# Block-sparse attention and a feed-forward layer: queries and choices transposed together by one DMA, two slots ahead

## The chip, the cores and the metric

The kernel runs on one core of a Trainium2 chip. The metric is the time of one execution on the device in microseconds (us); lower is better. TensorE (PE in the profile), VectorE (DVE), ScalarE (ACT), GpSimd (POOL) and SyncE (SP) each run their own instruction stream in program order; DMA transfers are issued from the queues of SP, ACT and POOL and run on 16 DMA engines.

## The reference

```
B, H, S, D = 4, 8, 768, 64;  chunks of 32 keys: nc = 24;  top_k = 6
k_min, k_max = min, max of k over each chunk
ub = sum over D of max(q * k_min, q * k_max)             # a bound for each query and chunk
ub = -1e9 where the chunk lies after the query's own chunk
top_chunks = the 6 chunks with the highest ub
scores = q @ k.T / sqrt(D), -1e9 outside the chosen chunks and after the query
attn = softmax(scores);  x = attn @ v                    # as 3072 tokens x 512
out = relu(x @ w_in) ** 2 @ w_out                        # w_in 512 x 2048, w_out 2048 x 512
```

## The kernel before

The work is cut into eight half batches (384 queries of one of the four batches, `ORDER`, so called hb below, 0 to 7), and each of them into four pairs of heads: 32 pairs, numbered from 0, `s = 4 * hb + p`. The Python loop over `slots` (one turn is called a slot here) writes every engine's instruction order out by hand; no scheduler moves anything. The short names of the code are steps of one pair:

- `step_P`: what the choice needs of the queries. Up to half batch 2 keys and queries are transposed on PE (`step_T`, L252); from half batch 3 on (`ON_PE = 3`) by DMA transposes into the tile `kqT` (`tr`, L305, three of 512 columns for k and three for q in each half batch), and `relus` (L301, L302) makes relu(-q) and relu(q) from it on DVE. The minima and maxima over key chunks come from `step_K` (L321, L327), cut into six parts that `k1()` lays into the slots.
- `step_U`: the bound ub on PE (L352, L356), the eight highest of each row on DVE (L363), and the choice (L364): a tile `nsel` with 1 for each chunk that is not chosen.
- `step_V`: `nsel` of two heads, 128 columns wide, is transposed on PE (L391, two or three 128x128 transposes) and copied by DVE into the query rows (L395, L396). The first four pairs have it together with the queries (L380, L385).
- `step_E`: scores. In the tile `kq` a head has 128 rows: 64 of queries or keys, and 64 where choices on the query side meet, on the key side, a code with -2^24 in the row of the key's chunk. One matmul (L409) thus gives the score and the mask; ACT takes the exponential (L414) and POOL cuts the diagonal blocks (L418).
- `step_F`: attention times v on PE (L434), divided by the sums into x on DVE (L443, L444).
- `step_X`: x of a whole half batch is transposed into `xT`, from half batch 2 to 6 by three DMA transposes on SP (L484), then `push` queues the feed-forward units: `ffn_up` (L524, L528, L530) and `ffn_down` (L540, and the output copy L546 on ACT). `f1()` takes the next unit from that queue; the slots are laid out with `f1()` calls between the attention's steps, so that PE always has something to run.

In a slot s of half batch 3 and later, the order is: (p = 0: `step_F` of the pair before, `step_X`), first scores of s, feed-forward units, `go(s, 2)` (two of the loads due), the other scores of the first head, `step_U(s + 1)`, `step_F(s - 1)`, scores of the second head, `step_V(s + 1)`, `go(s, 99)` (the other loads, `tr`, `place_dma`), the remaining scores, `step_P(s + 2)`, feed-forward units. `place_dma` (L291) copies keys and queries of a half batch from `kqT` into `kq`. Loads of q, k and v go through POOL's queue and are cast to bf16 on the way. SP's queue holds `tr`, x's transposes, `place_dma` and the outputs.

Of the kernel before, what the change touches and what calls it, by code (L numbers as in the profile page):

```python
# [39 lines left out]
def kernel(  # L40
# [36 lines left out]
    qn0 = consts.tile([128, HT, NP, 4, D], BF16, tag="qn0", name="qn")  # L77
# [3 lines left out]
    nsel = [consts.tile([128, HT, 2, D], BF16, tag=f"ns{i}", name="nsel") for i in range(3)]  # L81
    kbds = [consts.tile([128, NP, 2, 2, NC], BF16, tag=f"kbd{i}", name="kbd")
# [27 lines left out]
    def load_q0(h):  # L110
        nc.gpsimd.dma_start(
            out=qn0[:, :, h // 2, 1 + h % 2, :],
            in_=q[0, h, 0:HB].rearrange("(j p) d -> p j d", p=128))
# [39 lines left out]
    for h in (6, 7):  # L153
        load_q0(h)

    oneh = consts.tile([D, S], BF16, tag="oneh")
    nc.vector.tensor_scalar_mul(
        oneh.rearrange("p (c j) -> p c j", j=CH),
        ident[0:D, 0:NC].unsqueeze(2).to_broadcast([D, NC, CH]), OFFSEL)

    def codes(i, half, copy, p0=0, p1=NP):
        for h in range(2):
            copy(kqs[i][SROW[h]:SROW[h] + D, h, p0:p1, 2 * half, :],
                 oneh[:, HB * half:HB * half + HB].unsqueeze(1)
                 .to_broadcast([D, p1 - p0, HB]))

# [20 lines left out]

    def blank(p0, p1, c):

        nc.scalar.mul(qn0[:, :, p0:p1, c, :],  # L190
                      ident[:, 0:D].unsqueeze(1).unsqueeze(1)
                      .to_broadcast([128, HT, p1 - p0, D]), 0.0)

    def clear():

        for h in range(2):
            nc.vector.memset(kqs[1][SROW[h]:SROW[h] + D, h, :, 1, 0:128], 0.0)

# [31 lines left out]
    def step_cast(n, p):  # L230
        if n == "k":
            nc.vector.tensor_copy(packed("k", 0)[:, 2 * p:2 * p + 2], staged["k", p])
        else:
            nc.scalar.copy(qn0[:, :, p, 1:3, :], staged["q", p])

    def step_T(s, kp, qp, ns="kq"):

        b, half, p = slots[s]
        t = st.setdefault(s, {})
        for n in ns:  # L240
            pool, tag = kp if n == "k" else qp
            x = t[n] = pool.tile([128, HB], BF16, tag=tag, name="t" + n)
            if n == "q" and s < NP:
                for j in range(HT):
                    nc.tensor.matmul(
                        x[:, 128 * j:128 * (j + 1)],
                        lhsT=qn0[:, j, p, 1:3, :].rearrange("p h d -> p (h d)"),
                        rhs=ident, is_transpose=True, start=True, stop=True)
                continue
            for hh in range(2):  # L250
                for j in range(TP):
                    nc.tensor.matmul(  # L252
                        x[D * hh:D * hh + D, PP * j:PP * j + PP],
                        lhsT=packed(n, s // NP)[:, 2 * p + hh, D * j:D * j + D],
                        rhs=ident[0:PP, 0:PP], is_transpose=True, start=True, stop=True)
# [19 lines left out]
    def place(s, n, copy, h0=0, h1=2):  # L275
        b, half, p = slots[s]
        for h in range(h0, h1):
            copy(by_token(kqs[b % 2][QROW[h]:QROW[h] + D, h, p, 2 * half + "kq".index(n), :]),
                 in_order(st[s][n][D * h:D * h + D]))
# [67 lines left out]
    def step_U(s):  # L347
        b, half, p = slots[s]
        ncs = 12 * (half + 1)
        j0 = 1 - half  # L350
# [13 lines left out]
        nc.vector.tensor_tensor(  # L364
            (qn0[:, j0:, p, 0:4:3, 0:ncs] if s < NP else nsel[s % 3][:, j0:, :, 0:ncs]),
            ub, m8[:, j0:, :, TOPK - 1:TOPK].to_broadcast([128, HT - j0, 2, ncs]),
            op=ALU.is_lt)

    def qc(s, h):
        b, half, p = slots[s]  # L370
        return kqs[b % 2][:, h, p, 2 * half + 1, :]

    def step_V(s):
        b, half, p = slots[s]
        st[s]["e"] = [None, None]
        if s < NP:
            qt = psA.tile([128, 2, HB], BF16, tag="att", name="qt")
            for hh in range(2):
                for j in range(HT):
                    nc.tensor.matmul(  # L380
                        qt[:, hh, 128 * j:128 * (j + 1)],
                        lhsT=qn0[:, j, p, 2 * hh:2 * hh + 2, :]
                        .rearrange("p h d -> p (h d)"),
                        rhs=ident, is_transpose=True, start=True, stop=True)
            nc.vector.tensor_copy(kqs[b % 2][:, :, p, 2 * half + 1, :], qt)  # L385
            return
        j0 = 1 - half
        c = 128 * j0
        qt = psA.tile([128, HB], BF16, tag="att", name="qt")
        for j in range(j0, HT):  # L390
            nc.tensor.matmul(  # L391
                qt[:, 128 * j:128 * (j + 1)],
                lhsT=nsel[s % 3][:, j].rearrange("p h d -> p (h d)"),
                rhs=ident, is_transpose=True, start=True, stop=True)
        nc.vector.tensor_copy(qc(s, 0)[0:D, c:], qt[0:D, c:])  # L395
        nc.vector.tensor_copy(  # L396
            qc(s, 1)[D:128, c:], qt[D:128, c:])

    def step_E(s, hh, n):
# [7 lines left out]
        for (at, j, i0, m) in BANKS[half][n]:  # L407
            c = 128 * (i0 - HT * half)
            nc.tensor.matmul(  # L409
                ps[:, at:at + 128 * m],  # L410
                lhsT=kqs[b % 2][:, hh, p, 2 * (j // HT), 128 * (j % HT):128 * (j % HT + 1)],
                rhs=qc(s, hh)[:, c:c + 128 * m], start=True, stop=True)
# [11 lines left out]
    def step_F(s, hh):  # L424
# [13 lines left out]
        if hh == 1:  # L438
            if p == 0:
                xs[s // NP] = work.tile([128, HT, DM], BF16, tag="x", name="x")  # L440
# [3 lines left out]
            nc.vector.tensor_mul(  # L444
                x[:, :, 128 * p:128 * (p + 1)].rearrange("p j (h d) -> p h j d", h=2),
                po[:, :, :, 0:D], r.to_broadcast([128, 2, HT, D]))
            st.pop(s)

# [13 lines left out]
    def x_T(hb, g, pt, us=(0, 1)):  # L462
# [3 lines left out]
        for u in us:  # L466
            for j in range(HT):
                nc.tensor.matmul(
                    pts[hb, g][:, u, 128 * j:128 * (j + 1)],
                    lhsT=xs[hb][:, j, 128 * (2 * g + u):128 * (2 * g + u + 1)],  # L470
                    rhs=ident, is_transpose=True, start=True, stop=True)
# [4 lines left out]
    def step_X(hb, pe):  # L476
        xT = xT_of(hb)
        if pe:
            for g in range(2):
                x_T(hb, g, A)  # L480
                x_copy(hb, g, 0, 2, nc.scalar.copy if g else nc.vector.tensor_copy)
        else:
            for j in range(HT):
                nc.sync.dma_start_transpose(  # L484
                    out=xT[:, :, 128 * j:128 * (j + 1)], in_=xs[hb][:, j, :])
        push(hb)
# [46 lines left out]
    def ffn_down(hb, py, t, c, act, tail):  # L533
# [9 lines left out]
        if c == 3:  # L543
            ob = late.tile([128, DM], F32, tag="ob", bufs=3, name="ob")
            if act:
                nc.scalar.copy(ob, py[t])  # L546
# [50 lines left out]
    for g in range(ON_PE, 2 * B):  # L597
# [23 lines left out]
    step_cast("k", 0)  # L621
    blank(0, 1, 0)
    blank(0, 1, 3)
    step_cast("q", 0)
    blank(1, NP, 0)
    clear()
# [3 lines left out]
    step_T2(0)  # L630
    for h in range(2):

        nc.vector.memset(kqs[0][SROW[h]:SROW[h] + D, h, 2, 0, 0:1], 0.0)
    codes(0, 0, nc.sync.dma_start, 2, NP)
    place(0, "k", nc.scalar.copy)
    blank(1, NP, 3)
    step_U(0)
# [9 lines left out]
    extrema(st[1]["k"], 1)  # L647
    for i in range(3):
        nc.vector.memset(nsel[i], 0.0)
    early.close()  # L650
# [40 lines left out]
    for s, (b, half, p) in enumerate(slots):  # L691
# [6 lines left out]
        for fn, *a in first.get(s, ()):  # L698
            fn(*a)
        if ON_PE - 1 <= hb < 2 * B - 1 and p == (2 if hb < ON_PE else 1):  # L700
            parts.extend(step_K(hb + 1))
# [52 lines left out]
        if hb > 1 and s != 2 * NP:  # L754
            f1()
        go(s, 2)
        for n in range(hf, nb):
            step_E(s, 0, n)
        if hb < ON_PE and p:
            k1()  # L760
        if s + 1 < NS:
            step_U(s + 1)
        f1()
        if p and s > NP:
            step_F(s - 1, 0)
            step_F(s - 1, 1)
        if half == 0:
# [5 lines left out]
        f1()  # L773
        if s + 1 < NS:
            step_V(s + 1)
        k1()
        go(s, 99)
        for n in range(hf, nb):
            step_E(s, 1, n)
        k1()  # L780
        if s + 2 < NS:
            step_P(s + 2)
        f1()
        if half == 0:
# [41 lines left out]
```

## Time and profile before

| | |
|---|---|
| median of 3 runs | 278.38 us (276.56 to 282.24) |
| the profiled execution's own time | 278.13 us |
| its span, first to last instruction | 276.4 us |
| TensorE clock granted | 0.999 of full speed |
| DMA | 32.05 MB, 98,272 packets |

The profile is one execution. "Busy" is the time in which an engine had an instruction in work; waits of an engine are listed with the instruction that ended them; the chain is followed back from the last instruction. Rows of a timeline begin with the start and the duration in us. The prediction shows its lines where it uses them.

### The profile page before, as it was taken

The page shows a single profiled execution, that of the slowest core. Times are in us where ns is not written, and L with a number is a line of the kernel's source. Part 1 is how long each engine was busy: PE and PEld are TensorE (multiplying, and loading weights), DVE is VectorE, ACT ScalarE, POOL GpSimd, SP SyncE. Part 2 cuts the span into 40 slices and gives each one's busy share as a digit, 9 for nine tenths or more (in the row PEclk, how much of TensorE's full clock was granted, in tenths as well). Part 3 has the DMA queues.
Part 4 walks back from the last instruction along what each step waited for, and adds up shares of the span by engine and source line. Part 5 has one row for each costly group of instructions (what it writes and reads, how often), then busy time and mean ns, then how long its engine had stood idle before and what let it go on. Part 6 is the DMA issues. An engine that isn't in the chain of part 4 may idle for free.

```text
span 276.4 us, 6695 instructions
## 1 busy us (share of the span) xinstructions
PE 258.0 (93%) x2472; PEld 164.3 (59%) x2497; DVE 168.9 (61%) x647; ACT 181.9 (66%) x400; POOL 90.7 (33%) x135
## 2 busy tenths in 40 slices
PE   7887888899999999999999999999999999999994
PEld 6666555556666566655565566745565566655544
DVE  6878999666994368635884378615883455413411
ACT  5997879588975787835675777825674777625500
POOL 8695356316532017521551116701121111000000
PEclk9999999999999999999999999999999999999999
DMA  7999999959999259995699359997413200111002
GB/s 139 160 205 212 162 213 211 131 69 147 148 188 143 74 117 147 128 156 151 96 169 125 113 104 142 128 129 167 97 60 59 76 2 0 40 39 40 38 38 76
DMA packets 98272, 32.05 MB, mean 116 GB/s; under 512 B 84640, under 2 KB 93984, under 8 KB 98240
## 3 DMA queue, kind: packets, MB, share of 16 engines
q0 software_dynamic: 64688, 14.42, 66.6%
q1 hardware_dynamic: 32464, 16.88, 28.8%
q10 hardware_dynamic: 1088, 0.33, 0.5%
q8 instruction: 19, 0.31, 0.5%
q14 instruction: 13, 0.11, 0.1%
HBM read 27.26 MB, written 6.29 MB: 121 GB/s over the span
## 4 chain that ended last, share of the span: by engine, by line
PE 67%; DMA 9%; DVE 8%; ACT 7%; issue 3%; POOL 3%; SPq 1%; ACTq 0%; POOLq 0%; DVEq 0%
PE py L540 25%; PE ph L524 23%; PE ps L409 9%; PE po L434 7%; DMA vn<-in_v_dram 6%; ACT e L414 2%; ACT ht L528 2%; DVE h L530 2%; DMA xT<-x 2%; DVE km L321 1%; SPq L484 1%; DMA stage<-in_q_dram 1%; POOL e L418 1%; ACT ob L546 1%; PE ub L356 1%
## 5 line engine op out<-in xcount | busy, mean ns | idle before, releaser
L414 ACT ACTIVATE e<-ps 128x512 bf16<-128x512 f32 x192 | 97.1, 551 | 26.5 <-PE ps L409 26.5
L524 PE MATMUL ph<-xT,w_in 128*128 128x384 bf16 x512 | 99.2, 326 | 1.7 <-ACT ht L528 1.0
L540 PE MATMUL py<-w_out,h 128*128 128x512 bf16 x343 | 83.9, 379 | 2.6 <-ACT ob L546 0.9
L528 ACT ACTIVATE ht<-ph 128x384 bf16<-128x384 f32 x128 | 62.7, 500 | 27.5 <-PE ph L524 25.9
L418 POOL TENSOR_SCALAR_AFFINE_SELECT e<-e 128x384 bf16<-128x384 bf16 x64 | 34.1, 539 | 138.2 <-ACT e L414 138.2
L530 DVE TENSOR_TENSOR h<-ht 128x384 bf16<-128x384 bf16 x128 | 46.6, 376 | 43.9 <-ACT ht L528 43.6
L524 PEld LDWEIGHTS <-w_in 128*128 128x128 bf16 x512 | 47.5, 97 | 31.2 <-issue 2.4
L409 PE MATMUL ps<-kq 128*128 128x384 bf16 (+2 forms) x320 | 56.5, 278 | 1.8 <-DVE kq L395 0.8
L540 PEld LDWEIGHTS <-h 128*128 128x128 bf16 x368 | 34.9, 98 | 35.3 <-issue 1.7
L409 PEld LDWEIGHTS <-kq 128*128 128x128 bf16 x320 | 26.4, 98 | 14.5 <-issue 2.6
L434 PEld LDWEIGHTS <-e 128*128 128x128 bf16 x672 | 25.7, 98 | 6.7 <-issue 1.4
L363 DVE MAX8 m<-ub 128x8 f32<-128x24 f32 (+1 forms) x160 | 16.7, 171 | 20.3 <-PE ub L356 19.2
L434 PE MATMUL po<-vn,e 128*128 128x65 bf16 x672 | 27.1, 194 | 2.0 <-POOL e L418 0.8
L546 ACT COPY ob<-py 128x512 f32<-128x512 f32 x19 | 11.1, 586 | 22.7 <-PE py L540 22.3
L444 DVE TENSOR_TENSOR x<-po,r 128x384 bf16<-128x384 f32 x32 | 17.8, 558 | 1.1
L395 DVE COPY kq<-qt 64x384 bf16<-64x384 bf16 (+1 forms) x28 | 8.8, 315 | 12.4 <-PE qt L391 12.4
L105 POOL DMA_DIRECT2D kn<-in_k_dram x15 | 13.3, 891 | 0.6 <-DMA w_out<-in_moe_w_out_dram 0.4
L105 POOL DMA_DIRECT2D qn<-in_q_dram x15 | 13.3, 888 | 0.0
L321 DVE TENSOR_TENSOR km<-km 128x384 bf16<-128x384 bf16 (+3 forms) x40 | 11.3, 283 | 1.1
L356 PE MATMUL ub<-kbd,qr 128*128 128x48 bf16 (+1 forms) x160 | 9.5, 180 | 1.8 <-DVE kbd L219 0.8
L618 PE MATMUL idle<-ident 128*128 128x128 bf16 x97 | 8.7, 252 | 2.4 <-POOL ident masks.py:199 1.4
L121 POOL DMA_DIRECT2D vn<-in_v_dram x12 | 10.7, 904 | 0.4 <-issue 0.4
(68 smaller groups left out, 197.9 us busy)
## 6 DMA issues: line engine op xcount, KB each, us to landing
out_dram<-ob SPq DMA_DIRECT2D x23, 256.0 KB, 2.2
kq<-kqT SPq DMA_DIRECT2D x10, 384.0 KB, 5.2
w_in<-in_moe_w_in_dram POOLq DMA_DIRECT2D x2, 1024.0 KB, 13.2
w_out<-in_moe_w_out_dram POOLq DMA_DIRECT2D x2, 1024.0 KB, 19.7
kn<-in_k_dram POOLq DMA_DIRECT2D x15, 128.0 KB, 5.9
qn<-in_q_dram POOLq DMA_DIRECT2D x15, 128.0 KB, 7.0
vn<-in_v_dram POOLq DMA_DIRECT2D x12, 128.0 KB, 10.6
vn<-in_v_dram POOLq DMA_DIRECT2D x4, 384.0 KB, 7.8
```

The costliest lines, as they stand in the source:

```text
L105: nc.gpsimd.dma_start(out=nat_of(n, g)[:, DM * j:DM * j + DM].rearrange("p (h d) -> p h d", d=D), in_=rows(n, *ORDER[g], 0, H)[:, 128 * j: ...
L321: nc.vector.tensor_tensor(y, x[:, :, :, 0:m], x[:, :, :, m:2 * m], op=op)
L363: nc.vector.max(out=m8[:, j, hh, :], in_=ub[:, j - j0, hh, :])
L409: nc.tensor.matmul(ps[:, at:at + 128 * m], lhsT=kqs[b % 2][:, hh, p, 2 * (j // HT), 128 * (j % HT):128 * (j % HT + 1)], rhs=qc(s, hh)[:, c ...
L414: nc.scalar.activation(e[:, 512 * n + lo:512 * n + hi], ps[:, lo:hi], ACT.Exp, scale=float(scale))
L418: nc.gpsimd.affine_select(out=d, in_=d, compare_op=ALU.is_ge, fill=0.0, base=0, channel_multiplier=-1, pattern=[[0, 3], [1, 128]])
L434: nc.tensor.matmul(po[:, hh, i, :], lhsT=t["e"][hh][:, c:c + 128], rhs=vn[b % 2][:, 2 * p + hh, j, :], start=(j == 0), stop=(j == iq))
L444: nc.vector.tensor_mul(x[:, :, 128 * p:128 * (p + 1)].rearrange("p j (h d) -> p h j d", h=2), po[:, :, :, 0:D], r.to_broadcast([128, 2, HT ...
L524: nc.tensor.matmul(ph[:, 0:HB], lhsT=w_in[:, ki, 128 * f:128 * (f + 1)], rhs=xT[:, ki, :], start=(ki == 0), stop=(ki == NKI - 1))
L528: nc.scalar.activation(ht, ph[:, 0:HB], ACT.Relu)
L530: nc.vector.tensor_mul(h, ht, ht)
L540: nc.tensor.matmul(py[t], lhsT=h2[hb, f][:, 128 * t:128 * (t + 1)], rhs=w_out[:, f, :], start=(f == 0), stop=(f == NFI - 1))
```

## The change

In words, by parts:

- `kq` is laid out anew: both heads in rows 0 to 63 for queries and keys, and choices or codes in the 32 rows 64 to 95 (`CR`, `KR = 96`). Scores contract 96 rows. Code copies write 32 rows instead of 64.
- For pairs 0 to 3 queries and choices stand in 96 columns; queries are transposed head by head. For pairs 4 to 11 the choices (`chosen`) have 32 columns a head and are transposed on PE into 64 rows. Pair 12 has queries and choices transposed on PE together.
- For pairs 13 to 31 (14 on, counted from 1) `step_Q` copies the queries of the pair into `nsel` on DVE, `step_U` writes the choices beside them, and `step_W` transposes both by one DMA on SP, 768 columns, straight into `kq`. In slots from half batch 3 on, `step_U` and `step_W` are for the pair two slots ahead, `step_P` and `step_Q` for three ahead; at the end of slot 11 pair 13 is done in addition. `place_dma` carries only keys.
- x of half batches 2 to 6 is transposed pair by pair, 384 columns, from `step_F`.
- Moved: the q transposes one slot earlier; `go(s, 2)` in the slots from half batch 3 on falls away, so that all loads come at `go(s, 99)`; `step_K` at p = 0 instead of p = 1, with an extra `k1()` in half batch 2; in half batches 4 and 6, first and last slot, the `f1()` calls in the middle go to the slot's end. The output copy of the first token block of a half batch is split between DVE and ACT. Two small clears of `nsel` on DVE in slots 10 and 11.

The core of the diff:

```diff
-    QROW = (D, 0)
-    SROW = (0, D)
-    kqs = [consts.tile([128, 2, NP, 4, HB], BF16, tag=f"kq{i}", name="kq") for i in range(2)]
+    CR = CH
+    KR = D + CR
+    kqs = [consts.tile([128, NP, 4, 2, HB], BF16, tag=f"kq{i}", name="kq") for i in range(2)]
...
+    chosen = [consts.tile([128, HT, 2, CR], BF16, tag=f"ch{i}", name="chosen")
+              for i in range(2)]
+    nsel = [consts.tile([128, 2, 2, HT, 2, D], BF16, tag=f"ns{i}", name="nsel")
+            for i in range(2)]
...
             nc.sync.dma_start(
-                out=kqs[b % 2][QROW[h]:QROW[h] + D, h, :, 2 * half:2 * half + 2, :],
-                in_=half_T(g)[D * h:D * h + D])
+                out=kqs[b % 2][0:D, :, 2 * half, h, :],
+                in_=half_T(g)[D * h:D * h + D, :, 0, :])
...
+    def step_Q(s):
+        b, half, p = slots[s]
+        nc.vector.tensor_copy(
+            nsel[half][:, s % 2, :, :, 0, :],
+            nat["q", s // NP][:, 0:HT * DM]
+            .rearrange("r (j h d) -> r h j d", j=HT, h=H)[:, 2 * p:2 * p + 2])
+
+    def step_W(s):
+        b, half, p = slots[s]
+        nc.sync.dma_start_transpose(
+            out=kqs[b % 2][:, p, 2 * half + 1].rearrange("r h (j t) -> r (h j) t", j=HT),
+            in_=nsel[half][:, s % 2].rearrange("r h j n d -> r (h j n d)"))
...
         for j in range(j0, HT):
             nc.tensor.matmul(
-                qt[:, 128 * j:128 * (j + 1)],
-                lhsT=nsel[s % 3][:, j].rearrange("p h d -> p (h d)"),
+                qt[0:2 * CR, 128 * j:128 * (j + 1)],
+                lhsT=chosen[s % 2][:, j].rearrange("r h c -> r (h c)"),
                 rhs=ident, is_transpose=True, start=True, stop=True)
...
-                lhsT=kqs[b % 2][:, hh, p, 2 * (j // HT), 128 * (j % HT):128 * (j % HT + 1)],
+                lhsT=kqs[b % 2][0:KR, p, 2 * (j // HT), hh,
+                                128 * (j % HT):128 * (j % HT + 1)],
...
+            if 2 <= s // NP < 2 * B - 1:
+                nc.sync.dma_start_transpose(
+                    out=xT_of(s // NP)[:, p, :].rearrange("r (j t) -> r j t", j=HT),
+                    in_=x[:, p].rearrange("p j t -> p (j t)"))
...
-            if act:
+            if t == 0 and not tail:
+                nc.vector.tensor_copy(ob[:, 0:DM // 2], py[t][:, 0:DM // 2])
+                nc.scalar.copy(ob[:, DM // 2:], py[t][:, DM // 2:])
+            elif act:
...
             at(s0 - 1, tr, g, "k", j)
-            at(s0 + 1, tr, g, "q", j)
+            at(s0, tr, g, "q", j)
...
-        go(s, 2)
+        if hb < ON_PE:
+            go(s, 2)
...
-        if s + 1 < NS:
-            step_U(s + 1)
-        f1()
+        if s < NS - 2 or s + 1 == 3 * NP:
+            step_U(s + (1 if hb < ON_PE else 2))
+        if hb >= ON_PE and s < NS - 2:
+            step_W(s + 2)
...
+        late_f = half == 0 and hb > 2
+        if not (late_f and p in (0, NP - 1)):
+            f1()
...
-        if s + 1 < NS:
+        if hb < ON_PE:
             step_V(s + 1)
+        if ON_PE <= hb < 2 * B - 1 and p == 0:
+            parts.extend(step_K(hb + 1))
...
-        if s + 2 < NS:
+        if hb == ON_PE - 1:
+            k1()
+        if hb < ON_PE and s + 2 < NS:
             step_P(s + 2)
+            if s + 2 == ON_PE * NP:
+                step_Q(s + 2)
+        if s + 1 == ON_PE * NP:
+            f1()
+            step_Q(s + 2)
+            step_U(s + 2)
+            step_W(s + 2)
+        if hb >= ON_PE or s + 1 == ON_PE * NP:
+            if s + 3 < NS:
+                step_P(s + 3)
+                step_Q(s + 3)
```

More of the change, by code (lines that the diff above doesn't have):

```diff
@@ L186, with blank @@
     nc.scalar.activation(warm, ident[:, 0:1], ACT.Exp)
[L188 to L192, printed above, removed]
+    def blank(p0, p1):
+        for j in range(HT):
+            nc.scalar.mul(
+                qn0[:, j, p0:p1, :, D:KR].rearrange("p a h d -> p (a h) d"),
+                ident[:, 0:CR].unsqueeze(1).to_broadcast([128, 2 * (p1 - p0), CR]), 0.0)
     def clear():
         for h in range(2):
-            nc.vector.memset(kqs[1][SROW[h]:SROW[h] + D, h, :, 1, 0:128], 0.0)
+            nc.vector.memset(kqs[1][D:KR, :, 1, h, 0:128], 0.0)
     w_in = consts.tile([128, NKI, DFF], BF16, tag="w_in")
@@ L243, in step_T @@
             if n == "q" and s < NP:
[L244 to L248, printed above, removed]
+                for hh in range(2):
+                    for j in range(HT):
+                        nc.tensor.matmul(
+                            x[D * hh:D * hh + D, 128 * j:128 * (j + 1)],
+                            lhsT=qn0[:, j, p, hh, 0:D],
+                            rhs=ident, is_transpose=True, start=True, stop=True)
                 continue
@@ L277, in place @@
         for h in range(h0, h1):
-            copy(by_token(kqs[b % 2][QROW[h]:QROW[h] + D, h, p, 2 * half + "kq".index(n), :]),
+            copy(by_token(kqs[b % 2][0:D, p, 2 * half + "kq".index(n), h, :]),
                  in_order(st[s][n][D * h:D * h + D]))
@@ L348, in step_U @@
         b, half, p = slots[s]
+        st[s]["e"] = [None, None]
         ncs = 12 * (half + 1)
@@ L364, in step_U @@
         nc.vector.tensor_tensor(
-            (qn0[:, j0:, p, 0:4:3, 0:ncs] if s < NP else nsel[s % 3][:, j0:, :, 0:ncs]),
+            (qn0[:, j0:, p, :, D:D + ncs] if s < NP else
+             chosen[s % 2][:, j0:, :, 0:ncs] if s < ON_PE * NP else
+             nsel[half][:, s % 2, :, j0:, 1, 0:ncs].rearrange("p h j c -> p j h c")),
             ub, m8[:, j0:, :, TOPK - 1:TOPK].to_broadcast([128, HT - j0, 2, ncs]),
@@ L391, in step_V @@
             nc.tensor.matmul(
[L392 to L393 removed]
+                qt[0:2 * CR, 128 * j:128 * (j + 1)],
+                lhsT=chosen[s % 2][:, j].rearrange("r h c -> r (h c)"),
                 rhs=ident, is_transpose=True, start=True, stop=True)
[L395 to L397 removed]
+        for h in range(2):
+            nc.vector.tensor_copy(
+                kqs[b % 2][D:KR, p, 2 * half + 1, h, c:], qt[CR * h:CR * h + CR, c:])
     def step_E(s, hh, n):
@@ L630 @@
     step_T2(0)
-    for h in range(2):
-        nc.vector.memset(kqs[0][SROW[h]:SROW[h] + D, h, 2, 0, 0:1], 0.0)
+    nc.vector.memset(kqs[0][D:KR, 2, 0, :, 0:1], 0.0)
     codes(0, 0, nc.sync.dma_start, 2, NP)
     place(0, "k", nc.scalar.copy)
-    blank(1, NP, 3)
+    blank(1, NP)
     step_U(0)
@@ L647 @@
     extrema(st[1]["k"], 1)
-    for i in range(3):
-        nc.vector.memset(nsel[i], 0.0)
+    for i in range(2):
+        nc.vector.memset(chosen[i], 0.0)
     early.close()
@@ L699 @@
             fn(*a)
-        if ON_PE - 1 <= hb < 2 * B - 1 and p == (2 if hb < ON_PE else 1):
+        if hb == ON_PE - 1 and p == 2:
             parts.extend(step_K(hb + 1))
@@ L766 @@
             step_F(s - 1, 1)
-        if half == 0:
+        if half == 0 and not (late_f and p in (0, NP - 1)):
             f1()
@@ L772 @@
             step_E(s, 1, n)
-        f1()
-        if s + 1 < NS:
+        if not (late_f and p == 0):
+            f1()
+        if hb < ON_PE:
             step_V(s + 1)
+        if ON_PE <= hb < 2 * B - 1 and p == 0:
+            parts.extend(step_K(hb + 1))
         k1()
```

49 lines of the change are left out of this document (23 added, 26 removed).

## The prediction

> **What bounds the kernel now.** I read the page first: which engine is full, and what the chain that ended last is made of.
>
> ```profile
> PE 258.0 (93%) x2472; PEld 164.3 (59%) x2497; DVE 168.9 (61%) x647; ACT 181.9 (66%) x400; POOL 90.7 (33%) x135
> ...
> PE 67%; DMA 9%; DVE 8%; ACT 7%; issue 3%; POOL 3%; SPq 1%; ACTq 0%; POOLq 0%; DVEq 0%
> ```
>
> TensorE is busy 93% of the span and carries two thirds of the chain. An average over stages can mislead, so the second view is the table of windows, cut by stages: start-up with half batches 0 and 1; half batch 2 and the first pairs of 3; the rest up to half batch 7 (nearly all the pairs that the change is about, 13 to 31 counted from 0); and the tail of the feed-forward part.
>
> ```profile
> 0.00:60.00 60.00, 50.32 (x619) 35.23 (x622) 47.80 (x182) 47.12 (x110) 35.75 (x56) 1.00 1.52 171
> 60.00:104.00 44.00, 42.98 (x433) 27.80 (x437) 28.47 (x107) 33.90 (x74) 14.39 (x21) 1.00 1.14 133
> 104.00:244.00 140.00, 135.89 (x1257) 85.18 (x1272) 83.00 (x336) 91.15 (x198) 40.60 (x58) 1.00 0.87 103
> 244.00:276.00 32.00, 28.85 (x170) 16.04 (x169) 9.62 (x23) 9.78 (x20) 0.00 (x0) 1.00 0.14 50
> ```
>
> The columns after the length are busy time (and instructions) of PE, its weight loads, DVE, ACT and POOL, then the granted clock, the DMA share and GB/s. Between 104 and 244 us PE is busy 135.89 of 140.00 us at clock 1.00, while DVE and ACT have a third or more to spare. So a saving there counts in full only if it takes instructions off PE or takes away one of its few waits; anything added on DVE, SP or the DMA engines is free until it makes PE wait. Third view: PE's own waits from 60 to 244 us (total, times, longest).
>
> ```profile
> PE py L540 <- ACT ob L546: 0.9, 2, 0.5
> PE po L434 <- POOL e L418: 0.8, 2, 0.4
> PE ps L409 <- DVE kq L395: 0.6, 2, 0.3
> PE ph L524 <- DMA xT<-x: 0.6, 1, 0.6
> PE ub L356 <- DVE kbd L327: 0.5, 1, 0.5
> PE ub L356 <- DVE qr L301: 0.2, 1, 0.2
> ```
>
> Nine waits, 3.6 us. The view counts from the modelled end of the matmul before; the true loss is larger, as the timeline of one of them shows.
>
> ```profile
> 132.11 0.27 PE L391 MATMUL qt<-ident,nsel 128*128 128x128 bf16 x2
> 132.22 0.27 PE L409 MATMUL ps<-kq 128*128 128x256 bf16 x1
> 132.33 0.81 PE L524 MATMUL ph<-xT,w_in 128*128 128x384 bf16 x4
> 133.44 0.38 PE L409 MATMUL ps<-kq 128*128 128x384 bf16 x2 [0.30 <-DVE kq L395]
> ...
> 134.52 0.81 PE L524 MATMUL ph<-xT,w_in 128*128 128x384 bf16 x4
> 135.17 0.27 PE L409 MATMUL ps<-kq 128*128 128x256 bf16 x1
> ```
>
> From start to start, four ph matmuls take 0.65 us when nothing is late (134.52 to 135.17) and 1.11 before the wait (132.33 to 133.44): 0.46 us lost where the view says 0.30. With 0.16 added to each of nine waits the stretch loses 3.6 + 1.4 = 5.0 us. The whole of it is what better timing can give back.
>
> **The change part by part.**
>
> *Choices off PE.* For pairs 13 to 31 the PE transposes of L391 and the copies L395 and L396 go; one DMA transposes queries and choices together. The program order has two transposes for each of pairs 16 to 19 and 24 to 27 and three for the other eleven: 49. Two start 0.11 us ahead of what follows them (132.11 to 132.22), 0.055 each: 49 x 0.055 = 2.7 us off a full PE. Pair 12 keeps the PE way and has six transposes for three: +0.2.
>
> *Waits.* Choices two slots ahead instead of one remove the waits on kq and on qr. The remaining edits each stand at one of the listed waits: the first output copy of each half batch is split between DVE and ACT (py), feed-forward units are moved behind the last scores of a half batch (po on the select L418) and, in the following slot, behind all scores, x is transposed pair by pair, so that one small DMA and not three follow the last pair (ph), and the key extrema get an extra turn before pair 12 and an earlier start later (kbd). I take all 5.0 us. What covers them: the wait on the select was 0.4 us at its longest (0.56 with the 0.16), one feed-forward unit lasts 0.65 (134.52 to 135.17), and three units now stand there; between the two py groups there are now score matmuls of 0.1 to 0.4 us. If the cover is gone, a wait returns at 0.3 to 0.7 us each time.
>
> *Narrow transposes.* For pairs 4 to 11 the choices are 32 columns a head, so the PE transposes write 64 rows instead of 128. Such a narrow form exists before, at L252.
>
> ```profile
> 62.84 0.54 PE L409 MATMUL ps<-kq 128*128 128x128 bf16 x3
> 63.23 0.23 PE L352 MATMUL ub<-cmask,ident 128*128 128x144 bf16 x1
> ...
> 66.51 0.54 PE L409 MATMUL ps<-kq 128*128 128x128 bf16 x3
> 66.99 0.37 PE L252 MATMUL tk<-ident,kn 96*64 96x96 bf16 x8
> 67.18 0.36 PE L252 MATMUL tq<-ident,qn 96*64 96x96 bf16 x8
> 67.48 0.34 PE L524 MATMUL ph<-xT,w_in 128*128 128x384 bf16 x1
> ```
>
> The same three score matmuls last 0.39 us ahead of a full-width one and 0.48 ahead of a narrow one: entering costs 0.09. Eight narrow ones last 0.19 ahead of narrow ones and 0.30 ahead of a full one: leaving costs 0.11. Eight pairs x 0.20 = +1.6 us. Below it could be 0 where PE waits anyway (start-up), above it stays 1.6. The transposes of the first four queries become narrow too, but stand beside L252's narrow ones: 0.
>
> *Score matmuls over 96 rows.* All 320 at L409 now contract 96 rows, with 128 columns of weights as before. No row has this form. Bounds: 0 from the full form (only rows shrink) and, from L252, 0.20 for each entry and exit; four groups a pair in 32 pairs make 25.6 us. I take 0, since the row that costs has 64 columns as well as 96 rows, and the new form shares its 128 columns with the full one. [...]
>
> *DVE.* Two copies a pair leave, one copy of the queries (128x384, SBUF to SBUF) comes.
>
> ```profile
> L301 DVE TENSOR_SCALAR qr<-kqT 128x384 bf16<-128x384 bf16 x9 | 2.3, 256 | 0.1
> L396 DVE COPY kq<-qt 64x256 bf16<-64x256 bf16 x8 | 2.4, 295 | 0.3
> ```
>
> The nearest row for the new copy is 0.26 us, the old pair cost about 0.6: DVE gains 0.3 a pair, worth 0 since it waits for others. At the end of slot 11 the second pair ahead is filled in at once (a choice, two query copies, two relus, about 2 us of DVE in one place): 0 taken, at most +2.0 if a PE wait follows it.
>
> *SP and the DMA engines.* This is where the change can lose. SP issues in order.
>
> ```profile
> 143.11 3.95 SPq L305 DMA_TRANSPOSE kqT<-kn  x3
> 174.66 3.97 SPq L305 DMA_TRANSPOSE kqT<-kn  x3
> 180.41 4.88 SPq L484 DMA_TRANSPOSE xT<-x  x3
> kqT<-kn SPq DMA_TRANSPOSE x3, 8.4
> kqT<-qn SPq DMA_TRANSPOSE x15, 2.5
> 137.49 0.21 DVE L364 TENSOR_TENSOR nsel<-ub,m 128x48 bf16<-128x48 f32 x1
> 146.59 0.60 PE L409 MATMUL ps<-kq 128*128 128x384 bf16 x4
> 105.28 1.43 POOL L116 DMA_DIRECT2D vn<-in_v_dram  x1 [0.27 <-issue]
> 109.01 1.77 POOL L105 DMA_DIRECT2D kn<-in_k_dram  x2
> ```
>
> One 512-column transpose holds SP 3.97 / 3 = 1.3 us; the three of x, which now shrink to one of 384 columns behind the last pair, held it 4.88. Scaled by columns (an estimate; 1.3 to 2.6 are its ends) a 768-column one holds it 1.9 and x's 384-column one 1.0. Per half batch: 4 x 1.9 + 4 x 1.0 + 6 x 1.3 and some 2.5 of copies = 22 us, and a half batch lasts 174.66 - 143.11 = 31.6: it fits, but other transposes and output copies now stand ahead of a choice. Landing took 8.4 us where loads saturate the DMA engines (the row of the stretch 172 to 178 us) and 2.5 where they don't (the q transposes, over the whole span). The lead: the choice made in slot 18 is ready at 137.49 + 0.21 = 137.70, and pair 20, which will need it, starts its scores at 146.59: 8.9 us, the shortest lead I found. 8.4 against 8.9: no wait, with little room. Also, from half batch 3 on the loads are no longer issued in mid-slot (105.28) but with the rest (109.01), 3.7 us later, and the q transposes that wait for them come one slot earlier; SP can stand still there, with the next choice behind it. Taken as 0; the price is a rival's below. The code copies shrink from 64 to 32 rows a head, the key placement to half its bytes: less DMA work while it is short, 0 taken, perhaps 0.5 gained.
>
> *Sum:* -2.7 - 5.0 + 0.2 + 1.6 = -5.9 us. Against the profiled execution's 278.13 us (span 276.4): 272.2 us. Its own time is within 0.1% of the median 278.38, to which 272.2 is 2.2% less.
>
> **The rivals.**
>
> *Waits come back elsewhere.* PE's releasers are one step apart: a wait removed may be taken over by the next unit's. For it: the waits on kq and on ob are only 0.3 to 0.5 us each, so the next one is near. Against it: DVE and ACT had 57 and 49 us to spare in the 140, so nobody is late by habit. If three quarters of the 5.0 us return, 272.2 + 3.8 = 276.0, no measurable change.
>
> *The choices land late* (ends slower). Place: the scores of the pairs whose transposes meet loads, two in each of half batches 3, 4 and 5, or stand on SP behind a q transpose that waits for its load. If landing grows with columns, it takes 8.4 x 1.5 = 12.6 us against the lead of 8.9: 3.7 us for a pair, and half of that where the lead is longer. Six pairs lose 11 to 22 us: 283 to 294, and 285 as its value. It decides from a landing of about 9 us on. For it: the thin margin; against it: a median of 2.5 us outside the loads, and the fact that each wait gives the choices behind it that much more lead.
>
> [...] At 0.20 us for each of four groups a pair, 20 pairs in the full stretches give 16 us and all 32 give 25.6: 288 to 298. Against it: the columns, as said.
>
> That the change doesn't do what it says can be left out: the built program has the 19 new transposes and 49 fewer on PE for the same pairs.
>
> **How the numbers follow.** About 2% is what a measurement of this kernel can tell from no change, so the bound for faster is 272.8. Forecast 0.60, with its own range 269.5 to 275: 0.47 of it under the bound, since code copies and start-up can add to the gain, 0.13 above. Returned waits 0.16, all within 2%. Late choices 0.16, of which 0.13 slower. Mode change 0.08, slower. So faster 0.47, same 0.13 + 0.16 + 0.03 = 0.32, slower 0.13 + 0.08 = 0.21. The range runs from 269.5 to 284, which leaves out the mode change, the upper half of the late choices and little below.
>
> **What would show it.** Right: 19 transposes of 768 columns on SP, no PE transposes of choices after pair 12's; PE's waits from slot 13 on under 1.5 us; 0.2 us more around the transposes of pairs 4 to 11; weight loads of the scores no longer than before. Wrong: PE score matmuls waiting for the DMA that writes kq (late choices); gaps of 0.1 us on both sides of every score group (mode change); SP busy without pause, or its waits on q loads over 3 us; the first feed-forward unit of a half batch still waiting for xT, now behind a key transpose.

## The result: slower, by 12 to 16 us

The changed kernel takes 294.89 us (median of 6 runs, 289.18 to 297.24) against 278.87 us for the kernel before in the same session. That is 16 us by the medians, a ratio of 1.057. The ratio of the fast runs, two of the six (289.18 and 291.01), is 1.042 with a 95% interval from 1.032 to 1.052, some 12 us, and the profiled execution (294.79 us, its span 293.1) is one of the slower ones. The forecast was 272.2 us, the range ended at 284.0; every run lies above it.

First the engines on the changed kernel's page, then its window from 104 to 244 us and TensorE's waits from 60 to 244 us.

```profile
PE 261.7 (89%) x2438; PEld 163.0 (56%) x2463; DVE 163.2 (56%) x635; ACT 179.3 (61%) x402; POOL 91.0 (31%) x135
```

```profile
104.00:244.00 140.00, 123.31 (x1061) 74.70 (x1075) 72.03 (x297) 82.35 (x181) 39.76 (x56) 0.98 1.04 114
```

```profile
PE ph L549 <- DMA xT<-x: 9.9, 2, 5.4
PE ub L363 <- DVE kbd L333: 3.4, 4, 1.4
PE py L565 <- ACT ob L572: 1.7, 5, 0.4
PE po L460 <- POOL e L444: 1.2, 1, 1.2
PE ub L363 <- DVE qr L307: 0.5, 1, 0.5
PE py L565 <- issue: 0.2, 1, 0.2
```

Between 104 and 244 us TensorE is busy 123.31 us where it was 135.89, and the granted clock is 0.98 there instead of 1.00. Nine small waits, 3.6 us in all, have become fourteen, 16.9 us in all. The scores never wait for the new choices. What is waited for is another thing: the feed-forward units stand 9.9 us for xT, in two waits. The first of them, in the timeline, with what stood ahead of it on GpSimd, SP and VectorE:

```profile
113.05 2.64 POOL L109 DMA_DIRECT2D kn<-in_k_dram  x3
...
120.46 2.64 POOL L109 DMA_DIRECT2D qn<-in_q_dram  x3
...
121.26 0.56 DVE L470 TENSOR_TENSOR x<-po,r 128x384 bf16<-128x384 f32 x1
...
121.69 5.76 SPq L311 DMA_TRANSPOSE kqT<-kn  x3
...
127.99 1.18 SPq L474 DMA_TRANSPOSE xT<-x  x1
...
128.80 0.65 PE L549 MATMUL ph<-xT,w_in 128*128 128x384 bf16 x3
...
134.34 0.56 DVE L327 TENSOR_TENSOR km<-kqT 128x768 bf16<-128x768 bf16 x1 [8.89 <-DMA kqT<-kn]
...
134.86 0.48 PE L549 MATMUL ph<-xT,w_in 128*128 128x384 bf16 x1 [5.40 <-DMA xT<-x]
```

The x of pair 15, the last of half batch 3, is ready at 121.26 + 0.56 = 121.82 us. Its transpose is issued at 127.99, 6.2 us later. In between SP is at three key transposes of half batch 5. For two of them it waits until their loads have landed, 3.0 us in all by SP's waits from 119 to 128 us. Those loads were issued from 113.05 on, two of the three in the kernel before from 109.01 on (its row stands in the prediction); slot 14, to which they belong, begins 1.9 us later, so they are about 3 us later in their slot, and the first of them more. The other half of the delay is the order on SP. The same rows of the kernel before:

```profile
113.86 4.10 SPq L305 DMA_TRANSPOSE kqT<-kn  x3
119.61 4.64 SPq L484 DMA_TRANSPOSE xT<-x  x3
```

There the key transposes left SP at 113.86, and x, ready at 119.54, left at once. In the changed kernel the x of pair 14 has a transpose of its own on SP (117.91, for 1.54 us), and the key transposes stand behind it; so even without late loads they would be in work when the x of pair 15 comes. The view of DMA issues (KB or none, then us to landing) shows one more delay, x's transpose takes 6.8 us to land:

```profile
xT<-x SPq DMA_TRANSPOSE x1, 6.8
```

127.99 + 6.8 = 134.8 us, which is when TensorE goes on. From start to start the gap is 134.86 - 128.80 = 6.06 us for three matmuls of 0.16, so 5.6 us are lost; at the start of half batch 6 the same costs 4.6. Behind each gap the granted clock is one half for 3.4 us (0.51 in the second of these windows, 0.50 from 203.00 to 206.40 us), which loses about 1.7 us more each time (an estimate, half of the 3.4).

```profile
131.30:134.70 3.40, 0.00 (x0) 0.00 (x0) 0.36 (x1) 0.00 (x0) 0.00 (x0) 1.00 1.39 167
134.70:138.20 3.50, 3.34 (x12) 1.62 (x12) 2.51 (x12) 1.52 (x3) 0.00 (x0) 0.51 0.97 194
```

The account goes from pair 12's first score (87.75 us, 2.0 later than before) to pair 31's (248.23, 15.5 later): 10.2 for xT, 3.4 for the clock, 8.9 for the other twelve waits (7.0 by the view and 0.16 each), together 22.5; less the 5.0 us of waits before and 2.7 of transposes, 14.8. Measured: 160.5 us from the one to the other instead of 146.9, 13.6 more; the 1.2 between is not explained. This stretch, called the middle below, is a good measure for the other kernels too. The 2.0 us ahead of pair 12 come from slot 8, in which a stretch of half clock lies (0.50 from 49.40 to 52.80 us): it begins 1.1 us earlier than before and slot 9 1.0 later. Of the traces below some have such a stretch ahead of the middle and some don't (granted clock 0.94 to 0.97 from 0 to 60 us, or 1.00).

### The profile page after: what moved, and what is told of

It reads as the page before. It is cut to its first block, busy times and chain, and to the rows that moved or that the text cites. A ratio compares the mean times of both kernels' runs of the same rounds, so it can differ in the third digit from the quotient of the medians.

```text
span 293.1 us, 6657 instructions
## 1 busy us (share of the span) xinstructions
PE 261.7 (89%) x2438; PEld 163.0 (56%) x2463; DVE 163.2 (56%) x635; ACT 179.3 (61%) x402; POOL 91.0 (31%) x135
## 4 chain that ended last, share of the span: by engine, by line
PE 56%; DVE 14%; DMA 14%; ACT 5%; issue 4%; POOL 3%; SPq 2%; ACTq 0%; POOLq 0%; DVEq 0%
PE py L565 20%; PE ph L549 17%; PE ps L434 8%; DMA kn<-in_k_dram 7%; PE po L460 5%; DMA xT<-x 5%; DVE h L555 2%; PE idle L646 2%; ACT e L440 2%; DVE km L327 2%; DMA kq<-nsel 2%; SPq L311 2%; PE ub L363 1%; ACT ht L553 1%; DVE m L370 1%
## 5 line engine op out<-in xcount | busy, mean ns | idle before, releaser
L549 PE MATMUL ph<-xT,w_in 128*128 128x384 bf16 x512 | 102.1, 332 | 10.2 <-DMA xT<-x 9.9
L555 DVE TENSOR_TENSOR h<-ht 128x384 bf16<-128x384 bf16 x128 | 45.7, 367 | 58.5 <-ACT ht L553 58.1
L549 PEld LDWEIGHTS <-w_in 128*128 128x128 bf16 x512 | 48.4, 99 | 32.4 <-issue 4.0
L434 PE MATMUL ps<-kq 96*128 96x384 bf16 (+2 forms) x320 | 57.0, 280 | 1.7 <-DVE kq L410 1.3
L434 PEld LDWEIGHTS <-kq 96*128 96x128 bf16 x320 | 26.7, 98 | 27.1 <-issue 12.9
L572 ACT COPY ob<-py 128x256 f32<-128x256 f32 x7 | 2.6, 373 | 21.1 <-DVE ob L571 21.1
L327 DVE TENSOR_TENSOR km<-kqT 128x768 bf16<-128x768 bf16 x10 | 5.5, 552 | 16.9 <-DMA kqT<-kn 16.8
L571 DVE COPY ob<-py 128x256 f32<-128x256 f32 x7 | 3.0, 425 | 19.0 <-PE py L565 19.0
L574 ACT COPY ob<-py 128x512 f32<-128x512 f32 x12 | 7.0, 587 | 9.2 <-PE py L565 8.8
L363 PEld LDWEIGHTS <-qr 128*128 128x128 bf16 x160 | 7.9, 96 | 7.8 <-issue 3.5
```

The lines of the kernel that those rows point to most:

```text
L363: nc.tensor.matmul(ub[:, j - j0], lhsT=st[s]["qr"][:, w, 128 * j:128 * (j + 1)], rhs=kbds[b % 2][:, p, w, :, 0:ncs], start=False, stop=(j ...
L434: nc.tensor.matmul(ps[:, at:at + 128 * m], lhsT=kqs[b % 2][0:KR, p, 2 * (j // HT), hh, 128 * (j % HT):128 * (j % HT + 1)], rhs=qc(s, hh)[: ...
L549: nc.tensor.matmul(ph[:, 0:HB], lhsT=w_in[:, ki, 128 * f:128 * (f + 1)], rhs=xT[:, ki, :], start=(ki == 0), stop=(ki == NKI - 1))
L555: nc.vector.tensor_mul(h, ht, ht)
```

## Experiments

The theory (order and lead) is that the loads go out later, and the key transposes that wait for them stand on SP ahead of x; the same lateness holds VectorE at the key extrema, which the choices now need one slot earlier. There are two rivals: the new transposes overload SP and the DMA engines as such; or the loss is on TensorE (96 rows, narrow transposes). For every run the median is given, then the ratio to the kernel before with its 95% interval.

**Loads half a slot earlier, in the changed kernel.**

```diff
-        if hb < ON_PE:
+        if hb < ON_PE or p > 1:
             go(s, 2)
```

> The changed kernel, with only the loads of slots 14, 15, 18, 19, 22 and 23 back in mid-slot (two of them ahead of the second half of the first head's scores). Order theory (the x transpose of the last pair stands on SP behind key transposes that wait for loads issued 4 to 6 us later than before): SP waits under 4.5 us instead of 5.8 at the key transposes of slot 15, x of pair 15 is issued near 124 us instead of 128, the two waits for xT of 5.4 and 4.5 us shrink to under 1 each, no half clock behind them, the waits on kbd mostly go: 281 to 285 us (1.01 to 1.02 of before). Rival, the new transposes of choices load SP and the DMA engines too much: the waits for xT stay over 3 us, over 289 us. Rival, the losses are on PE itself (96 rows, narrow transposes): no difference, 290 to 295.

Measured: 286.76 us, 1.033 (1.024 to 1.041). TensorE's waits:

```profile
PE ph L549 <- DMA xT<-x: 5.6, 2, 3.0
PE ub L363 <- DVE kbd L333: 3.6, 4, 1.5
```

8 us of the median come back, the middle loses 5.1 us instead of 13.6, and no half clock is left in it (granted clock 1.00 from 104 to 244 us). But that is less than the theory asked for: its 281 to 285 was missed, the waits for xT shrink without going, and those on kbd stay. The rows of SP and of the issues say why:

```profile
116.88 1.41 SPq L474 DMA_TRANSPOSE xT<-x  x1
118.38 4.49 SPq L311 DMA_TRANSPOSE kqT<-kn  x3
123.40 2.21 SPq L474 DMA_TRANSPOSE xT<-x  x1
```

```profile
xT<-x SPq DMA_TRANSPOSE x1, 8.0
```

x leaves at 123.40 instead of 127.99 (1.0 of it because its slot begins earlier) but needs 8.0 us to land instead of 6.8, still amid the loads of q. So there are two delays, the place in the queue and the landing, and this edit mends only a part of the first: no key transpose waits for its load any more, but the three still start right behind pair 14's x, at 118.38 where they started at 113.86 in the kernel before, and hold pair 15's x, ready at 120.55, for 2.9 us. That part of the delay comes from the new order on SP and not from late loads.

**x ahead of the key transposes, loads as late as in the changed kernel.**

```diff
-            at(s0 - 1, tr, g, "k", j)
...
             step_X(hb - 1, False)
+            for j in range(HT if hb < 2 * B - 1 else 0):
+                tr(hb + 1, "k", j)
```

> The changed kernel with late loads, but the three key transposes are issued right behind the last pair's x at the start of the next slot instead of ahead of it. Order theory: x goes as soon as it is ready, the waits for xT fall under 1 us and the half clock behind them goes; the keys still land as late or a little later, so VectorE still stands at the key extrema (about 9 us) and the waits on kbd (1.5 each in slots 17 to 18 and 25 to 26) stay or grow: 283 to 288 us. If instead the DMA engines are simply short, x lands late wherever it stands in the order: waits for xT over 3 us, 290 or more.

Measured: 292.07 us, 1.048 (1.040 to 1.055). The time is that of the second case, the mechanism is not: xT is waited for 1.7 us in all, not over 3 each. Two of TensorE's waits, VectorE's wait for the keys (104 to 244 us) and x on SP:

```profile
PE ub L363 <- DVE qr L307: 9.3, 3, 4.7
...
PE ph L549 <- DMA xT<-x: 1.7, 2, 0.9
```

```profile
DVE km L327 <- DMA kqT<-kn: 23.1, 3, 10.1
```

```profile
120.52 1.18 SPq L474 DMA_TRANSPOSE xT<-x  x1
```

The waits for xT are nearly gone as the theory says, though this x, which leaves as soon as it is ready (120.49), takes 8.4 us to land: when x leaves at once, a long landing is waited for by 0.9 us at most. Nearly as many microseconds have moved to qr, and the two stretches of half clock, which were expected to go, now come with the waits on it (from 135.7 and 204.0 us; granted clock 0.98 from 104 to 244 us). VectorE stands 10.1 us at the key extrema (L327), and the relu that makes qr (L307) is behind them on the same engine. Order alone changes who waits.

**Both edits together.**

> Both edits: loads early and x ahead of the key transposes. Order theory: neither xT nor the key extrema are waited for; what is left over the kernel before is the start (slots 8 to 12, 2 to 3 us) less 2 to 4 of the forecast gain: 278 to 283 us. Rivals: as for the single edits, 288 or more.

Measured: 286.45 us, 1.029 (1.022 to 1.035): outside the expected 278 to 283, because VectorE still waits for the keys (17.2 us in three waits, 7.0 the longest). Of TensorE's waits xT keeps 0.5 us, and the largest is now:

```profile
PE ub L363 <- DVE qr L307: 4.9, 3, 2.7
```

**Late loads alone, in the kernel before.**

```diff
-        go(s, 2)
+        if hb < ON_PE:
+            go(s, 2)
```

> The kernel before, with only the loads from half batch 3 on issued with the rest of a slot's jobs instead of two of them in mid-slot. If the late loads alone make the loss, the same chain appears without any transposed choice: SP waits some 4 to 6 us at the key transposes, xT is waited for at slots 16 and 24 by 3 to 5 us each: 284 to 290 us (1.02 to 1.04). If the late loads hurt only together with the new transposes on SP (x by pairs, choices in between), 278 to 281: not measurable.

Measured: 289.13 us, 1.038 (1.032 to 1.045). This one part of the change costs 10 us without any transposed choice. In the trace the middle loses 10.7 us, half clock behind the waits included (granted clock 0.96 from 104 to 244 us); 2.7 more lie ahead of it, with a granted clock of 0.97 from 0 to 60 us, where the edit changes nothing. TensorE's longest wait, then the timeline of SP and TensorE:

```profile
PE ph L524 <- DMA xT<-x: 6.9, 2, 4.5
```

```profile
119.33 5.48 SPq L305 DMA_TRANSPOSE kqT<-kn  x3
124.90 5.48 SPq L484 DMA_TRANSPOSE xT<-x  x3
...
134.31 1.44 PE L524 MATMUL ph<-xT,w_in 128*128 128x384 bf16 x4 [4.50 <-DMA xT<-x]
```

The chain is that of the changed kernel: key transposes late, x behind them, TensorE 4.5 us at rest. So late loads are enough for such a loss, without any of the new transposes; that the new order adds to it, the first experiment showed.

**Loads a whole slot earlier, in the changed kernel.**

```diff
-            at(8 * b - 2 + g, load_v, b, 4 * g, 4 * g + 4)
+            at(8 * b - 3 + g, load_v, b, 4 * g, 4 * g + 4)
...
-            at(4 * g - 6 + i // HT, load_n, "kq"[i // HT], g, i % HT)
+            at(4 * g - 7 + i // HT, load_n, "kq"[i // HT], g, i % HT)
```

> The changed kernel with the loads of q, k and v from half batch 4 on issued one whole slot earlier (slots 9, 10, 13, 14, 17, 18, 21, 22), still at the end of the slot. Lead theory (choices two slots ahead pull the key extrema, and so the key transposes and their loads, forward by most of a slot, while the loads went back by half a slot): with the loads a slot earlier neither xT nor the key extrema nor qr are waited for: in the stretch from slot 16 to slot 28 the loss of 14 us falls to 1 to 2, and the time to 279 to 282 us. Rival (x by pairs and choices on SP are themselves the obstacle): SP's queue is as full as before, waits for xT of 2 to 3 us remain as with the loads half a slot earlier: 284 to 287. Rival (the earlier loads meet other transfers): new waits of the scores for the choices' transposes, 284 or more.

Measured: 279.40 us, 1.005 (1.001 to 1.008). TensorE's two largest waits, SP's rows and x's landing:

```profile
PE ub L363 <- DVE kbd L333: 3.1, 4, 1.4
PE py L565 <- ACT ob L572: 1.7, 5, 0.4
```

```profile
119.49 5.36 SPq L311 DMA_TRANSPOSE kqT<-kn  x3
125.37 1.64 SPq L474 DMA_TRANSPOSE xT<-x  x1
```

```profile
xT<-x SPq DMA_TRANSPOSE x1, 4.1
```

By the medians 15.5 of the 16 us are back with the order on SP unchanged, the middle is 1.4 us shorter than in the kernel before, and no wait for xT is listed. x still leaves at 125.37, later than with the loads half a slot earlier, but lands in 4.1 us, when the loads of q are nearly over: their queue moves 0.00 MB from 125.3 to 126.0 us, and 0.07 MB from 123.3 to 124.0 in the kernel with the loads half a slot earlier. Neither rival can be the cause by itself, since all the new transposes, the 96 rows and the narrow form are in this kernel. These loads are earlier than in the kernel before, though: the new order needs more lead than the old one. The waits on kbd remain, so for them the lead was not the cause.

**The same loads in the kernel before,** by the same two lines.

> The kernel before with its loads a whole slot earlier. Its waits for loads were one of 0.6 us only, so at most 1 us is to be had: 277 to 279 us, no measurable change. If the kernel before was itself held by its loads in a way that its waits did not show, 274 or less.

Measured: 279.05 us, 1.002 (0.999 to 1.005). It gains nothing, so what the earlier loads give back in the changed kernel is what the change had taken.

**The output copy whole, on top of the earlier loads.** The two lines for DVE and ACT go, `elif act` becomes `if act`.

> The same with the first output copy of a half batch whole again on ScalarE. If the split copy runs one half after the other (0.42 + 0.37 us against 0.59), the six waits of py on it (1.9 us in all) shrink to the two of the kernel before (0.9): 1 to 2 us under the kernel with the earlier loads. If the split is not what delays it, no difference.

Measured: 277.09 us, 0.995 (0.991 to 0.999), 2.3 us less, somewhat above the expected. The waits on the copy are gone (1.7 us by the view). In the two traces the middle differs by only 0.7 us, since 0.6 us of waiting for xT has come in. In the changed kernel's groups the two halves take 0.37 and 0.42 us, and the one on ACT starts only when that on DVE is done; whole, the copy takes 0.59. Why the second half waits for the first is not shown. The rows of the changed kernel:

```profile
L572 ACT COPY ob<-py 128x256 f32<-128x256 f32 x7 | 2.6, 373 | 21.1 <-DVE ob L571 21.1
...
L571 DVE COPY ob<-py 128x256 f32<-128x256 f32 x7 | 3.0, 425 | 19.0 <-PE py L565 19.0
...
L574 ACT COPY ob<-py 128x512 f32<-128x512 f32 x12 | 7.0, 587 | 9.2 <-PE py L565 8.8
```

**The choices of pairs 4 to 11 with 64 columns a head again,** so that the transposes write 128 rows:

```diff
-                qt[0:2 * CR, 128 * j:128 * (j + 1)],
-                lhsT=chosen[s % 2][:, j].rearrange("r h c -> r (h c)"),
+                qt[:, 128 * j:128 * (j + 1)], lhsT=wide(s % 2)[:, j],
...
```

> The same with the choices of pairs 4 to 11 64 columns a head again, so that their PE transposes have the full form. By the trace of the changed kernel the narrow form costs 0.09 to 0.10 us on each side of a group, 8 groups: 1.6 us less, all of it from slot 3 to slot 11; if PE waits there for something else anyway, nothing: 0 to 1.6 under the kernel with the earlier loads and the whole copy.

Measured: 276.55 us, 0.995 (0.991 to 0.998): 0.5 us less than the run before it, which these runs do not separate from nothing. By the starts of the scores, slots 9 and 10 take 0.33 us less (0.17 a pair), slot 8 takes 0.22 less and slots 4 to 7 only 0.07 in all.

**An extra turn for the key extrema.** `if hb == ON_PE - 1: k1()` at the end of a slot becomes `if hb >= ON_PE - 1: k1()`.

> The changed kernel with its loads a whole slot earlier, the output copy whole, the choices of pairs 4 to 11 of 64 columns, and one extra turn for the key extrema at the end of each slot, so that the last of them no longer stands right ahead of the choice that needs it. If the four waits on kbd (3.2 us) are only a matter of that turn, they go and nothing else takes their place: 273 to 274.5 us, 0.98 to 0.985 of before. If the key transposes' landing sets them, or VectorE has no room one slot earlier, they stay or turn into waits on qr: 276 to 277.

Measured: 275.32 us, 0.986 (0.981 to 0.990): under both kernels, by 1.4% under the one before and so within the 2%. TensorE's waits from 60 to 244 us:

```profile
PE ub L366 <- DVE qr L310: 1.2, 3, 0.4
PE ph L551 <- DMA xT<-x: 0.4, 1, 0.4
PE ps L436 <- DMA kq<-kqT: 0.2, 1, 0.2
PE py L567 <- issue: 0.2, 1, 0.2
```

kbd is gone and qr has taken 0.8 us of its place: 2.0 us in all, where the kernel before had 3.6. It misses the 273 to 274.5 by a little, since the gain over the kernel without the turn is 1.2 of the 3.2 us by the medians of two sessions, and 1.9 by the middle of the two traces.

**From that version, the feed-forward units at their old places** (`late_f = False`), **and x's four transposes all behind the last pair.**

> The same without the moved feed-forward units (in the first and last pair of half batches 4 and 6 they stand at their old places). As forecast, two waits of po on the select come back, 0.4 to 0.6 us each, and perhaps one of xT: 0.5 to 2 us more. If the moved units hid nothing, no difference.

> The same, but the four transposes of x of a half batch are all issued behind its last pair. SP then needs four times 1.2 us instead of one for what the feed-forward part waits for: xT is waited for by 1 to 4 us at slots 16 or 17 and 24 or 25: 1 to 6 us more. If x by pairs was worth nothing (four units of the half batch before and the scores cover it), no difference.

Measured: 276.38 us, 0.990 (0.987 to 0.994), and 276.53, 0.992 (0.989 to 0.995). They are 1.1 and 1.2 us above the version that has both, with intervals that overlap, so neither gain is certain; the waits that return are those that the expectations named. At the old places po waits for the select (and py 0.9 us for the output copy); with x together xT is waited for 1.9 us instead of 0.4:

```profile
PE po L462 <- POOL e L446: 1.1, 2, 0.6
```

```profile
PE ph L552 <- DMA xT<-x: 1.9, 4, 0.6
```

## Why the prediction was wrong

- **The step that failed** is "SP can stand still there, with the next choice behind it. Taken as 0". The standstill came, 3.0 us of it ahead of pair 15's x, but I named the wrong victim, the choice, which has two slots of lead. The x of the last pair stands behind the same key transposes with no lead at all: it left SP 6.2 us after it was ready, took 6.8 to land, and cost 10.2 us in two waits and 3.4 of half clock. The prediction had its cost among the gains ("one small DMA and not three follow the last pair") and costed the SP queue by how much it holds in a half batch (22 us of 31.6), not by who is at its end when a load is late, or when one more x goes ahead of the key transposes. The list of signs had it right, "now behind a key transpose", but no rival and no price stood for it.
- **The price was not visible in the waits before.** In the kernel before the chain load, key transpose, x, feed-forward unit had 0.6 us of wait in all, so it looked free. The late loads in the kernel before show that it was at its end: loads 3 to 4 us later in their slot gave two waits of 6.9 us together, half clock behind them, and 10.7 us in the middle. Moving the loads was counted as a row of SP and not followed to its last reader.
- **The lead of the key extrema.** Choosing two slots ahead needs kbd a slot earlier, so VectorE reaches the extrema earlier while the keys come later; it stood 8.9 us. The prediction listed the earlier start only as a removed wait. What it should have compared is the date of the load with the date of its first reader, both of which the change moves, towards each other.
- **Waits, -5.0.** 16.9 us by the view instead of 3.6. The split copy, counted as a gain, runs one half behind the other and cost 2.3 us by the medians. The moved feed-forward units and x by pairs do what was said once the loads are in time: about 1.1 us each, at the edge of what these runs can tell.
- **Transposes off TensorE, -2.7.** Right as far as it can be seen: from pair 28's first score to pair 31's the kernel before takes 24.84 us and the one with earlier loads and the whole copy 24.18, 0.66 less for three pairs where 9 x 0.055 = 0.50 was forecast. The rows are theirs, before first:

```profile
207.85 0.32 PE L409 MATMUL ps<-kq 128*128 128x384 bf16 x1
...
232.69 0.38 PE L409 MATMUL ps<-kq 128*128 128x384 bf16 x2
```

```profile
206.79 0.38 PE L434 MATMUL ps<-kq 96*128 96x384 bf16 x2
...
230.97 0.49 PE L434 MATMUL ps<-kq 96*128 96x384 bf16 x3
```

- **Narrow transposes, +1.6.** 0.17 us a pair in the full stretch against 0.20; in the start-up TensorE waits for other things anyway (4.0 us listed from 20 to 60 us with the narrow form), and the two medians differ by 0.5 us in all.
- **Rivals.** "Choices land late" was the right place (SP, loads, half batches 3 to 5) with the wrong tile, and its 285 was too low; the choices' own transposes landed in 2.8 us at the median (8.7 at most), and no score waited for them. The third, called "mode change" in the chances, a price of 0.20 us for every group of scores on 96 rows, fell, though the time lies in its 288 to 298: the kernel with earlier loads has all its scores on 96 rows and takes 279.40, and their weight loads take 98 ns with 128 rows (before) and with 96 (after; the longer idle time ahead of them falls to 16.6 us with the earlier loads). No run shows a mode that changes; the 0 taken for 96 rows was the author's estimate from the columns, and the only price of a form that the rows show is the 0.09 and 0.11 us around the narrow one.

```profile
L409 PEld LDWEIGHTS <-kq 128*128 128x128 bf16 x320 | 26.4, 98 | 14.5 <-issue 2.6
```

```profile
L434 PEld LDWEIGHTS <-kq 96*128 96x128 bf16 x320 | 26.7, 98 | 27.1 <-issue 12.9
```

- **The half clock** was in no term. In the changed kernel 3.40 us with 0.00 us of TensorE's work (from 131.30) are followed by 3.50 us at 0.51, and 3.40 us with 0.00 (from 199.60) by 3.40 us at 0.50.

With the loads in time, the whole copy, wide choices and the extra turn, the rest of the change is worth 3.5 us of the forecast 5.9.

## What to carry to other kernels

When a load or a transfer is issued later, follow every queue that it holds up to the last thing behind it, and ask what that thing's reader has in hand; a wait of 0.6 us before says nothing of how near the edge the chain is (here late loads alone made it 6.9). When a result is wanted a slot earlier, its whole chain of inputs must move a slot earlier too, and putting the victim ahead in the queue may only pass the wait to the next engine, as it did here (1.7 us left on xT, 9.3 on qr). The halves of the copy split between two engines ran one behind the other here, 0.42 and 0.37 us against 0.59 whole; look at what releases the second.

## What the runs showed of the hardware

- The clock fell not only behind a full rest. In the changed kernel stretches of half clock begin at 49.41, 134.74 and 203.01 us and last 3.41 us each; their starts are 85.33 and 68.27 us apart, 25.0 and 20.0 times that length, and why is not shown. The 3.40 us ahead of the second and the third hold 0.00 us of TensorE's work, those ahead of the first 2.25. With the loads half a slot earlier TensorE works 0.42 us in 3.40 (from 128.00), and no half clock follows. So the work in the 3.4 us ahead, as the view counts it, does not decide it alone; what else counts is left open. The rows are the changed kernel's, then the one with the loads half a slot earlier:

```profile
46.00:49.40 3.40, 2.25 (x33) 1.59 (x34) 2.44 (x7) 2.11 (x6) 0.80 (x2) 1.00 3.45 130
49.40:52.80 3.40, 3.18 (x18) 1.56 (x19) 2.58 (x7) 1.49 (x4) 2.24 (x3) 0.50 1.66 87
```

```profile
128.00:131.40 3.40, 0.42 (x3) 0.13 (x2) 0.92 (x3) 0.56 (x1) 0.00 (x0) 1.00 1.77 215
```

- A DMA transpose held SP 1.18 us for 384 columns (127.99) when nothing blocked it, much as for 512 (1.3 in the prediction). The prediction's estimate by columns, 1.0 for 384 and 1.9 for 768, was off: the nineteen transposes of choices, 768 columns each, held it 1.21 us at the least and 1.25 at the median.
